# Block-selected causal attention feeding a gated convolution unit: convolution on four column groups of the array, fp16 high/low bounds, row-half scores, and a list-scheduled order

## The chip, the cores and the metric

The kernel runs on one NeuronCore of one Trainium2 chip. The metric is the device time of one execution in microseconds, the median over repeated executions. The profile gives the span from the first to the last instruction of one profiled execution, which is a little shorter than the time.

## The reference, cut to what matters

Inputs are `q`, `k`, `v` of shape (4, 8, 768, 64), a value matrix and an output matrix of 512 x 512, and a 5-tap depthwise filter `conv_w` (5, 512), all fp32. First comes attention with chunk selection: for each query, an upper bound of its score with each chunk of 32 keys is formed, and only the six chunks with the largest bounds take part. Its output `x` (4, 768, 512) then goes through a causal depthwise convolution, whose sigmoid gates `x @ w_val`, and through `w_out`.

```python
k_min, k_max = k_chunks.min(3), k_chunks.max(3)             # 24 chunks of 32 keys
ub = sum_d maximum(q * k_min, q * k_max)                    # (.., 768, 24), future chunks -1e9
top_chunks = argsort(ub)[..., -6:]
scores = q @ k.T / 8 ; masked to chosen chunks and to keys at or before the query
attn = softmax(scores) @ v
x = heads side by side                                      # (4, 768, 512)
gate = sigmoid(sum_k conv_w[k] * x shifted by k-4)
out = (gate * (x @ w_val)) @ w_out
```

## The kernel before, in words

Two heads make a pair, so there are 16 pairs (`NPAIR`), four per batch. The two heads of a pair lie side by side in the 128 partitions of transposed tiles: 64 rows of head dimension each.

Per pair the work is cut into steps, each a small function that issues its instructions:

- `kq_steps`: TensorE turns K and Q (fp32, 128 x 128 pieces, L155 and L178) so that the head dimension lies on the partitions; ScalarE writes fp16 copies with zero rows beside them (L159, L181, with GpSimd's casts L183); VectorE takes each chunk's maximum and minimum (L163, L164) and makes the small fp32 bound matrix `KB` (L167 to L172); GpSimd casts V (L190).
- `sel_steps`: the bounds are two fp32 matmuls per query tile of 128 (L207, L209), using `max(q*kmin, q*kmax) = q*kmin + relu(q)*(kmax-kmin)`; VectorE adds the causal fill, takes the top eight and compares with the sixth (L211 to L224); the "not chosen" matrix is turned (L233) and copied into spare rows of the query tile `QU` (L236).
- `attn_steps`: the scores are one matmul per head and key tile (L271, L291). The stationary operand holds 64 rows of keys and, in other rows, the chunk indicator times -30, so that the mask is added by the same matmul. It uses 88 or 128 rows of the array for one head at a time. ScalarE takes the exponential (L275, L295), GpSimd zeroes the upper triangle of diagonal blocks (L264, L280), TensorE multiplies by V with an extra column of ones (L304), VectorE normalises (L306, L307), and the result is turned into `xT` (L314, L316).
- `moe_gate`, `moe_val`, `moe_out`: for each of the 16 channel groups of 128 the depthwise convolution is done as matmuls with diagonal 128 x 128 matrices, five taps times a high and a low fp16 part, on each half of 384 positions: 20 matmuls (L334), then tanh (L339). The value product (L348), gating (L352), output product (L359), eviction (L362) and store (L363) follow per batch.

The order on every engine is the order in which the steps are issued. `merge` interleaves attention of pair i, selection of pair i+1, K/Q work of pair i+2 and the gate work of earlier pairs by equal fractions of each list:

```python
keyed += [((j + 0.5) / n, li, j, s) for j, s in enumerate(steps)]
...
merge(attn_steps(i),
      sel_steps(i + 1) if i + 1 < NPAIR else [],
      kq_steps(i + 2) if i + 2 < NPAIR else [],
      moe[i])
```

Loads of pair i+2 are issued ahead of each merge on the SyncE queue, 192 KB per head and tensor in rows of 256 bytes. Eight DMAs of this queue are in flight at most, since each waits for the one eight before it.

The softmax here doesn't subtract the row's maximum and nothing guards it: scores larger than these inputs give would overflow.

## Time and profile before

| quantity | value |
|---|---|
| time, median of 2 runs | 294.5 us (294.18 to 294.82) |
| span of the profiled execution | 292.5 us |
| mean granted TensorE clock | 0.959 |
| first score matmul (L271) starts | 27.07 us |
| last output matmuls (L359) start, span ends | 283.13 us, 292.5 us |
| DMA moved | 28.46 MB, queue 1 at 40.9% of 16 engines |
| convolution L334, busy | 57.8 us, 320 matmuls |
| bounds L207 and L209, busy | 31.2 and 32.3 us, 160 records each |
| scores L271, busy | 54.9 us, 224 matmuls |

A matmul's record includes the time in which it passes through the array, and records overlap, so a group's busy time and the mean of one matmul overstate what it costs in a stream. The distance from the start of one group to the start of the next is what the stream pays; the timeline gives it. Each engine works its own queue in order.

### The profile page before, as it was taken

The numbers are of one execution on the slowest core, as the hardware profiler recorded it, in microseconds if no ns is written. First come the engines' busy times: TensorE is split into PE (matmuls) and PEld (weight loads), VectorE is DVE, ScalarE is ACT, GpSimd is POOL, SyncE is SP. The second block draws the span as 40 slices with busy tenths as digits, with TensorE's granted clock in tenths as the row PEclk, the third lists the DMA queues.
The fourth block names the chain that finished last, engine by engine and source line by source line (L and its number), as shares of the span: only waits on it lengthen the run. The fifth ranks groups of instructions, "written<-read, shape, count | busy, mean of one in ns | idle before, by whom it ended". The sixth has DMA issues, their size and how long they took to land.

```text
span 292.5 us, 5928 instructions
## 1 busy us (share of the span) xinstructions
PE 241.3 (82%) x2161; PEld 171.6 (59%) x2161; DVE 155.2 (53%) x522; ACT 160.2 (55%) x329; POOL 121.8 (42%) x261
## 2 busy tenths in 40 slices
PE   2383926509998897999998999999989999999994
PEld 1181614405757575776666667676757676765551
DVE  3547162404676674858573657666645667631160
ACT  3232713503768659465674774756747765467313
POOL 2416189999254436243433253425251624223000
PEclk9999975956999999999999999999999999999999
DMA  7999992205162554242456343332211000003105
GB/s 165 211 304 245 218 175 54 54 0 110 33 132 55 110 110 99 66 108 56 107 151 159 91 114 86 70 87 61 74 74 38 36 2 0 2 2 143 73 2 215
DMA packets 80746, 28.46 MB, mean 97 GB/s; under 512 B 75962, under 2 KB 76622, under 8 KB 80718
## 3 DMA queue, kind: packets, MB, share of 16 engines
q1 hardware_dynamic: 80718, 28.09, 40.9%
q8 instruction: 17, 0.28, 0.4%
q14 instruction: 11, 0.09, 0.1%
HBM read 21.79 MB, written 6.29 MB: 96 GB/s over the span
## 4 chain that ended last, share of the span: by engine, by line
PE 66%; POOL 12%; ACT 10%; issue 3%; SPq 3%; DVE 2%; DMA 2%; ACTq 0%; POOLq 0%
PE ps_w L334 17%; PE ps_s L271 10%; POOL diag L379 7%; PE ps_av L304 6%; PE ps_w L348 6%; PE ps_w L359 6%; PE ps_w L209 6%; ACT P L275 5%; PE ps_w L207 5%; PE ps_w L155 4%; PE ps_w L178 2%; POOL QU L183 2%; PE ps_w L314 2%; ACT KE L159 2%; ACT osb L362 1%
## 5 line engine op out<-in xcount | busy, mean ns | idle before, releaser
L275 ACT ACTIVATE P<-ps_s 128x512 f16<-128x512 f32 x160 | 87.8, 606 | 57.1 <-PE ps_s L271 56.8
L271 PE MATMUL ps_s<-QU,KE 88*128 88x512 f16 (+5 forms) x224 | 54.9, 336 | 7.1 <-ACT P L275 4.1
L264 POOL TENSOR_SCALAR_AFFINE_SELECT P<-P 128x256 f16<-128x256 f16 (+1 forms) x80 | 29.0, 364 | 71.1 <-ACT P L275 58.3
L334 PE MATMUL ps_w<-xT,diag 128*128 128x384 f16 x320 | 57.8, 331 | 0.0
L304 PE MATMUL ps_av<-VA,P 128*128 128x65 f16 x672 | 33.4, 196 | 21.9 <-POOL P L264 19.9
L304 PEld LDWEIGHTS <-P 128*128 128x128 f16 x672 | 28.4, 99 | 32.0 <-POOL P L264 26.2
L159 ACT ACTIVATE KE<-ps_w 64x384 f16<-64x384 f32 x64 | 31.0, 485 | 26.9 <-PE ps_w L155 26.5
L183 POOL CAST QU<-q 64x384 f16<-64x384 f32 x64 | 35.1, 548 | 24.6 <-ACT q L181 22.7
L334 PEld LDWEIGHTS <-diag 128*128 128x128 f16 x320 | 31.0, 99 | 21.4 <-issue 1.9
L339 ACT ACTIVATE g<-ps_w 128x384 f32<-128x384 f32 x32 | 15.9, 498 | 30.5 <-PE ps_w L334 30.5
L209 PE MATMUL ps_w<-KB,q 128*128 128x48 f32 x160 | 32.3, 285 | 0.0
L163 DVE TENSOR_REDUCE kmx<-ps_w 128x12 f32<-128x384 f32 x32 | 17.8, 555 | 26.7 <-ACT KE L159 26.6
L236 DVE COPY QU<-ps_w 24x640 f16<-24x640 f16 x32 | 15.5, 484 | 29.9 <-PE ps_w L233 29.4
L207 PE MATMUL ps_w<-KB,rq 128*128 128x48 f32 x160 | 31.2, 278 | 0.0
L271 PEld LDWEIGHTS <-KE 88*128 88x128 f16 (+1 forms) x224 | 21.1, 101 | 16.8 <-issue 10.8
L280 POOL TENSOR_SCALAR_AFFINE_SELECT P<-P 128x256 f16<-128x256 f16 x32 | 13.1, 408 | 31.4 <-ACT P L275 31.3
L207 PEld LDWEIGHTS ps_w<-KB,rq 128*128 128x128 f32 x160 | 25.9, 202 | 0.3
L155 PE MATMUL ps_w<-ident,kn 128*128 128x128 f32 x96 | 17.7, 300 | 9.7 <-DMA kn<-in_k_dram 9.7
L209 PEld LDWEIGHTS ps_w<-KB,q 128*128 128x128 f32 x160 | 25.7, 202 | 0.0
L348 PE MATMUL ps_w<-xT,wval_sb 128*128 128x384 f16 x128 | 23.9, 325 | 1.8 <-ACT q L181 1.8
L190 POOL CAST VA<-vn 128x384 f16<-128x384 f32 x32 | 16.5, 516 | 20.4 <-PE ps_av L304 12.9
L359 PE MATMUL ps_w<-wout_sb,gv 128*128 128x512 f16 x96 | 23.8, 379 | 0.7 <-ACT osb L362 0.7
(46 smaller groups left out, 309.0 us busy)
## 6 DMA issues: line engine op xcount, KB each, us to landing
kn<-in_k_dram SPq DMA_DIRECT2D x32, 192.0 KB, 3.3
qn<-in_q_dram SPq DMA_DIRECT2D x32, 192.0 KB, 3.4
vn<-in_v_dram SPq DMA_DIRECT2D x32, 192.0 KB, 3.3
out_dram<-osb SPq DMA_DIRECT2D x24, 256.0 KB, 2.0
w<-in_moe_w_val_dram SPq DMA_DIRECT2D x1, 1024.0 KB, 5.6
w<-in_moe_w_out_dram SPq DMA_DIRECT2D x1, 1024.0 KB, 7.9
KE<-echunk SPq DMA_DIRECT2D x6, 96.0 KB, 2.7
cfill<-cfill SPq DMA_DIRECT2D x1, 120.0 KB, 2.3
```

What stands on the lines that cost most here:

```text
L155: nc.tensor.transpose(out=pt[:, tl * 128:(tl + 1) * 128], in_=kn[:, 3 * w + tl, :], identity=ident)
L159: nc.scalar.activation(out=ke[HP[hh], hh, sl], in_=pt[HP[hh]], func=AF.Copy, scale=0.125)
L183: nc.gpsimd.tensor_copy(out=qu[HP[hh], hh, sl], in_=q32[HP[hh], sl])
L207: nc.tensor.matmul(out=pu[:, it - 1, :], lhsT=rq[:, ts], rhs=kb[:, 0, :], start=True, stop=False)
L209: nc.tensor.matmul(out=pu[:, it - 1, :], lhsT=q32[:, ts], rhs=kb[:, 1, :], start=False, stop=True)
L264: nc.gpsimd.affine_select(out=ap, in_=ap, pattern=[[0, n], [1, 128]], compare_op=ALU.is_ge, fill=0.0, base=0, channel_multiplier=-1)
L271: nc.tensor.matmul(out=pq[:, col:col + n], lhsT=ke[KP[hh], hh, jt * 128:(jt + 1) * 128], rhs=qu[KP[hh], hh, q0:q0 + n], start=True, stop=True)
L275: nc.scalar.activation(out=pt, in_=pq, func=AF.Exp)
L304: nc.tensor.matmul(out=pav[:, qt, :], lhsT=where[hh, jt, qt], rhs=va[:, hh, jt, :], start=(jt == 0), stop=(jt == qt))
L334: nc.tensor.matmul(out=pg, lhsT=diag[:, ki * NCT + ct, part, :], rhs=xT[:, slot, w * HB + ki:w * HB + ki + HB], start=(n == 0), stop=(n == ...
L348: nc.tensor.matmul(out=pv, lhsT=wval_sb[:, ct, et * 128:(et + 1) * 128], rhs=xT[:, slot0 + ct, 4 + w * HB:4 + (w + 1) * HB], start=(ct == ...
L359: nc.tensor.matmul(out=po, lhsT=gv[b, et][:, s * 128:(s + 1) * 128], rhs=wout_sb[:, et, :], start=(et == 0), stop=(et == NCT - 1))
```

## The change

The change replaces the hand-written merge by a graph of operations with modelled durations and a list scheduler, and at the same time recasts three pieces of TensorE's work.

**Bounds.** Q is scaled by 64 and split into an fp16 high part `Qh` and low part `ql`; their positive parts are `rh` and `rl`. The bound matrix is split likewise, high and low side by side (96 columns). A query tile now takes four fp16 matmuls of 96 columns instead of two fp32 matmuls of 48. VectorE makes `ql`, `rh`, `rl` and adds the two halves of the product (`bsum`, twice); the bound matrix is made by seven small GpSimd instructions (`ksmall`).

**Scores.** The stationary operand holds only a head's 64 rows. Head 0 lies in rows 0 to 63 and head 1 in rows 64 to 127 of the array; their matmuls are issued in turn, to two banks. The mask is a second matmul from the indicator `E` and the turned selection `MT`, accumulated on the same bank, for queries from 192 on. ScalarE evicts K and Q with one instruction per half, both heads at once.

**Convolution.** A shifted copy of `xT` is made through DRAM: one DMA writes `xT` of a pair to `scr`, four DMAs read it into `XS` so that 32 channels lie in each quarter of the partitions, with the quarters holding shift and part (high or low) variants. A matmul then has 32 output columns, and the four groups of 32 channels go to four column groups of the array. Three shifts times four groups give 12 matmuls of 384 positions per half, 24 per pair instead of 20.

**Order.** Every operation has a key, `p * PERIOD + OFF[stage]`; on each engine the scheduler starts the ready operation with the smallest key, given modelled durations, a free bank of the eight, and the buffers of `NBUF`. The resulting order is what each engine's queue holds. Constants are made on the chip rather than loaded; the two weight matrices are loaded by GpSimd with a cast; eight matmuls on zeros are issued first.

In the resulting queues the first operations are these. SyncE: the loads of K, Q, V of pairs 0, 1 and 2, then the filter, then pair 3. TensorE: the zeros; K and Q of pairs 0 and 1; bounds of pair 0; K and Q of pair 2; bounds of pair 1; the turn of the filter; the turn of pair 0's selection; scores of pair 0. At the end, after the turn of the last pair's output, TensorE has 52 value matmuls, 96 convolution matmuls and 48 output matmuls left.

```diff
-    def merge(*lists):
...
+PERIOD = 9.537
+OFF = dict(load=-38.8, ktr=-26.25, qtr=-23.06, kev=-7.55, qev=-7.41, ksm=-26.91, spl=-1.52, vc=6.87,
...
+    def key(stage, p, x=0.0):
+        return p * period + off[stage] + x
...
+    G.op("cw", "SP", 2.0, kd + off["load"] + 2 * period, w_cw, w=[("cw4",)], lat=4.0)
...
+            G.op(f"{name}{p}", "SP", 1.1, key("load", p, x + (3 if x == 2 else 0)), load(name), w=[(name, p)], lat=3.2)
...
+        def rhi(p=p):
+            t.nc.vector.tensor_scalar(out=vv("rh", p), in0=vv("Qh", p)[:, 128:S], scalar1=0.0, scalar2=None,
+                                      op0=ALU.max)
+
+        def rlo(p=p):
+            t.nc.vector.scalar_tensor_tensor(out=vv("rl", p), in0=vv("Qh", p)[:, 128:S], scalar=0.0,
+                                             in1=vv("ql", p), op0=ALU.is_gt, op1=ALU.mult)
...
+                terms = [(vv("rh", p)[:, sl], 0), (vv("rl", p)[:, sl], 0), (vv("Qh", p)[:, sq], 1),
+                         (vv("ql", p)[:, sl], 1)]
+                for k, (lhsT, m) in enumerate(terms):
+                    t.nc.tensor.matmul(out=b[:, i * 96:(i + 1) * 96], lhsT=lhsT,
+                                       rhs=kb[:, m].rearrange("p a c -> p (a c)"), start=(k == 0), stop=(k == 3))
...
+                    for hh in range(2):
+                        nc.tensor.matmul(out=bb[hh][:, col:col + n], lhsT=kh[HP[hh], jt * 128:(jt + 1) * 128],
+                                         rhs=qh[HP[hh], q0:q0 + n], start=(si == 0), stop=(last and not masked),
+                                         skip_group_check=True)
+                    if masked:
+                        for hh in range(2):
+                            nc.tensor.matmul(out=bb[hh][:, col + m0 - q0:col + n],
+                                             lhsT=t.E[HP[hh], jt * 128:(jt + 1) * 128],
+                                             rhs=mt[HP[hh], m0 - 128:q0 + n - 128], start=False, stop=last,
+                                             skip_group_check=True)
...
+        def xw(p=p):
+            t.nc.sync.dma_start(out=t.scr[p % 4].rearrange("c (g n) -> g c n", g=4), in_=t.xT[:, p % 8, :])
+
+        def xs(p=p):
+            n = 4 * XW
+            for blk in range(4):
+                sh = 3 * (blk // 2)
+                t.nc.sync.dma_start(out=vv("XS", p)[32 * blk:32 * blk + 32, 0:n - 3], in_=t.scr[p % 4][:, sh:sh + n - 3])
...
+                for o in range(3):
+                    for g in range(4):
+                        t.nc.tensor.matmul(out=b[32 * g:32 * g + 32, 0:HB], lhsT=t.WD[:, o * 16 + (p % 4) * 4 + g, :],
+                                           rhs=x[:, g * XW + w * HB + o:g * XW + w * HB + o + HB], start=(o == 0), stop=(o == 2))
...
+    with tc.manual_schedule():
+        for o in order:
+            o.emit()
```

## The prediction

> **What bounds the kernel now.** I read the page first, for the engine that is busiest and for the chain that ended last.
>
> ```profile
> span 292.5 us, 5928 instructions
> PE 241.3 (82%) x2161; PEld 171.6 (59%) x2161; DVE 155.2 (53%) x522; ACT 160.2 (55%) x329; POOL 121.8 (42%) x261
> ...
> PE   2383926509998897999998999999989999999994
> ...
> PE 66%; POOL 12%; ACT 10%; issue 3%; SPq 3%; DVE 2%; DMA 2%; ACTq 0%; POOLq 0%
> ```
>
> TensorE is the bound: from about a third of the span on its slices are full, and it holds 66% of the chain. So the next question is what each kind of matmul costs there. For that I take the timeline of TensorE in the steady stage, and read the distance between starts, not the durations, which overlap.
>
> ```profile
> 157.29 2.28 PE L334 MATMUL ps_w<-xT,diag 128*128 128x384 f16 x13
> 159.41 0.50 PE L314 MATMUL ps_w<-identh,onat 128*128 128x128 f16 x6
> 159.74 0.38 PE L271 MATMUL ps_s<-QU,KE 88*128 88x512 f16 x1
> ...
> 160.51 0.32 PE L207 MATMUL ps_w<-KB,rq 128*128 128x48 f32 x2
> ...
> 162.68 1.03 PE L359 MATMUL ps_w<-wout_sb,gv 128*128 128x512 f16 x4
> 163.54 0.60 PE L271 MATMUL ps_s<-QU,KE 88*128 88x512 f16 x3
> 163.98 0.49 PE L155 MATMUL ps_w<-ident,kn 128*128 128x128 f32 x3
> 164.31 0.38 PE L271 MATMUL ps_s<-QU,KE 88*128 88x512 f16 x1
> ...
> 167.26 0.68 PE L304 MATMUL ps_av<-VA,P 128*128 128x65 f16 x16
> 167.78 0.38 PE L271 MATMUL ps_s<-QU,KE 128*128 128x512 f16 x1
> ```
>
> A convolution matmul takes (159.41 - 157.29)/13 = 163 ns, an fp16 turn 55 ns, one pair's bounds 162.68 - 160.51 = 2.17 us, an output matmul 215 ns, an fp32 turn 110 ns, an attention-times-V matmul 32.5 ns. Those of 384 and 512 columns come to 0.42 ns a column, and I use this for all wide ones. Per pair: turns of K and Q 12 x 0.11 = 1.32; bounds 2.17; turn of the selection 0.28; scores 5376 columns x 0.42 = 2.26; times V 42 x 0.0325 = 1.37; turn of the output 0.34; convolution 20 x 0.163 = 3.26; value 8 x 0.163 = 1.31; output 6 x 0.215 = 1.29. Sum 13.6 us. The chain in order of time gives the true period:
>
> ```profile
> 144.98 0.86 PE ps_w L359 x4
> ...
> 204.92 0.86 PE ps_w L359 x4
> ```
>
> These are the same step of two batches, four pairs apart: 59.94/4 = 14.98 us. So TensorE gives 13.6/14.98 = 0.91 of its time to the stream. I take this for the new kernel too; a planned order might do better, three nearly equal engines worse.
>
> The start is read from the timeline of the first 30 us.
>
> ```profile
> 14.19 0.88 PE L155 MATMUL ps_w<-ident,kn 128*128 128x128 f32 x3 [4.53 <-DMA kn<-in_k_dram]
> 24.12 2.07 POOL L366 CAST wval_sb<-w 128x2048 f16<-128x2048 f32 x1
> 24.36 2.04 DVE L185 TENSOR_SCALAR rq<-q 128x384 f32<-128x384 f32 x1
> 27.07 2.35 PE L271 MATMUL ps_s<-QU,KE 88*128 88x512 f16 x7 [1.86 <-DVE QU L236]
> ```
>
> TensorE stands 4.53 us for pair 1's keys while pair 0's bounds are queued behind them. The first score comes at 27.07. VectorE's L185, whose mean is 0.59 us, took 2.04 us beside a GpSimd cast.
>
> **What the Trainium skill says.** (1) TensorE: Matmul & The Clock Gate, Measured speedup vs the span model: four row tiles ran 3.07 times and three column tiles 2.38 times as fast as one after another. No matmul of this trace is tiled, so it neither confirms nor denies it. (2) TensorEngine Tiling (Array Packing), Key Properties: changing the tiling mode drains the engine. Not seen here either. (3) SBUF — State Buffer, Who interferes with whom: VectorE in a two-port mode, or with two inputs in SBUF against a GpSimd instruction that reads SBUF, waits until the other has ended. The 2.04 us beside the 2.07 us above agrees.
>
> **The change part by part.** All per pair on TensorE unless said.
>
> Bounds: 20 fp16 matmuls of 96 columns. Between 32.5 ns at 65 columns and 55 ns at 128 lies 44 ns, so 0.88 us for 2.17.
>
> Scores: 2688 columns per head as before, plus 2432 for the mask from query 192 on, 5120 per head. If the two row halves run side by side: 5120 x 0.42 = 2.15; one after another: 4.30; the skill's efficiency (about 0.8 of the tiles' number) would give 2.69. I take 2.2: its packs stood alone, so that fixed times weigh, while here matmuls follow in a stream.
>
> Convolution: 24 matmuls for 20. Four at a time: 24 x 0.163/4 = 0.98; at 3.07: 1.27; serial: 3.91. I take 1.0 for the same reason.
>
> Mode changes: the queue goes into and out of the row or column form some ten times a pair. A record of 331 ns at a distance of 163 says that about 0.17 us is passage through the array, so a drain costs 0 to 0.17: 0 to 1.7 a pair. I take 0.3, most being small beside the waits that the 0.91 already holds.
>
> The rest, unchanged: 1.32 + 0.28 + 1.37 + 0.34 + 1.31 + 1.29 = 5.91. Sum: 5.91 + 0.88 + 2.2 + 1.0 + 0.3 = 10.3 us against 13.6, or 165 us in all.
>
> The other engines, per pair. ScalarE: eight exponentials of 512, two of 384, two of 256, four evictions and two tanh of 384, one and a half evictions of 512. Five L275 in 2.56 us give 0.51 each back to back, and two L181 0.87, or about 0.4 each: in all 8.7; at record durations (606, about 500, 386 ns) 10.5. Splitting each head's K eviction (L159, 485 ns x4) is gone. VectorE: four reductions 2.2 (555 and 548 ns), `ql` 0.9, `rh` and `rl` 1.2, two sums 0.8 (L211 408 ns), ten MAX8 0.86, compare 0.43, selection copy 0.48, reciprocal and normalising 1.47, output copy 0.56, gating 1.09: 10.0 at record durations, about 8.7 back to back. GpSimd: about 4.8; seven small instructions of `ksmall` bounded by the 178 ns memset (L129, 96 columns) and the 294 ns select (L264, 128 columns) of the groups by shape. All lie beside TensorE as long as it is at 10.3. The new wait on GpSimd is for chunk maxima, with casts and triangles queued behind it; bounds wait for it two pairs ahead of need.
>
> DMA:
>
> ```profile
> 8.00:16.00 8.00, 2.89 (x13) 2.35 (x13) 2.98 (x10) 1.99 (x5) 3.16 (x6) 1.00 1.10 214
> ...
> 225.00:240.00 15.00, 14.52 (x141) 10.56 (x140) 8.60 (x28) 10.61 (x24) 6.54 (x15) 1.00 0.10 36
> ```
>
> The last two columns are the share of DMA time and GB/s. The 256-byte loads saturate at 214 GB/s, the stores' larger packets at 36/0.10 = 360. Loads 1.18 MB: 5.5 us; the copy through DRAM 0.99 MB: 2.75 at 360, 4.6 at 214; stores 0.39 MB: 1.1. Together 9.4 to 11.2, but loads are done well before the end, so it is hidden by 10.3/0.91 = 11.3.
>
> Start: before the filter stand 18 loads, 3.54 MB. At 214 GB/s they end near 17.5 us; at the rate at which pair 1's keys came (2.33 MB in 13 us, 180 GB/s) near 20.6. The turn of pair 2's keys and of the filter stand on TensorE ahead of pair 0's selection. The filter lands then at 20 to 22; with the turn, VectorE's split and the selection copy (about 2 us) the first score starts at about 24, 3 us earlier than now. Dropping 0.6 MB of constants is the gain; the order, planned with 1.1 us for two loads where 214 GB/s needs 1.8, gives much of it back. Before it TensorE has done 36 turns, two bounds, one selection: 6 us.
>
> End: after the last turn TensorE has 52 x 0.163 + 4 x 1.0 + 48 x 0.215 = 22.8 us of work, so the round trip through DRAM (two transfers of some 2 to 3.3 us each, by the rows of stores and loads) is hidden behind values and outputs. After the last output matmul there is an eviction and a store: now 292.5 - 288.3 = 4.2 us. The time is 2.0 over the span.
>
> Forecast: 24 + (165 - 6)/0.91 + 4.2 + 2.0 = 205 us.
>
> **Rivals.**
> A, tiles do not overlap: 10.3 - 2.2 - 1.0 + 4.30 + 3.91 = 15.3 a pair; (245 - 6)/0.91 + 30.2 = 293; with drains at 0.17 (another 1.4 a pair) 317, slower than before. For it: nothing in this trace runs two matmuls at once. Against: the skill's measurements.
> B, VectorE becomes the bound: record durations 10.0 plus 1 us of holding by GpSimd (three exposed instructions, about 0.3 each, as GpSimd is busy nearly half the time and an instruction lasts 0.4 to 1.0) is 11.0; less 14 us done before the first score and 4 in the tail, (176 - 18)/0.91 = 174; 24 + 174 + 22.8 + 6.2 = 227. For it: L185's 2.04 us. Against: in the busiest 30 us VectorE now does 21 us without being waited for.
> C, the planned order keeps TensorE fuller: perfect tiling, no drains, 0.95: 10.0 x 16 = 160; 154/0.95 + 30.2 = 192. For it: nothing wide is left in one piece. Against: the plan's load times are too short, and TensorE's queue waits in order for a late operand, as the 4.53 us show.
>
> **How the numbers follow.** Forecast 0.60, B 0.20, C 0.14, A 0.06. The likeliest is 205. The range goes from 188, a little under C, to 230, a little over B; only A and a few tails lie outside. Slower takes half of A and unknowns: 0.04; same the 293 side of A: 0.03; faster 0.93.
>
> **What would show it.** Right: distance between starts of two-head scores near 0.42 ns a column for both heads together; 12 convolution matmuls in 0.5 to 0.65 us; a pair's 20 bound matmuls in 0.9; period near 11.3; first score near 24 with TensorE waiting on the filter's load. Wrong: if the score group of a pair takes over 4 us (A), if TensorE waits mostly on VectorE (B), or if transfers through `scr` are what SyncE's queue waits for while loads stand behind them.

## The result, and the profile after

The changed kernel takes 235.9 us (median of 2 runs, 234.8 to 237.0), where the kernel before takes 294.5 us. The ratio is 0.800, with a 95% interval from 0.789 to 0.810. It is faster, as forecast, but 31 us slower than the 205 us forecast and outside the range of 188 to 230. The ratios in this document are formed from executions in the fast state alone, which matters most for the run with six output tiles, where three of six executions were slow and the fast ones took 231.4 to 233.9 us.

The page of the changed kernel: span, busy time of the engines, slices of TensorE, of its granted clock and of DMA, queue 1, and the chain that ended last.

```profile
span 233.1 us, 7133 instructions
...
PE 191.0 (82%) x2713; PEld 129.4 (56%) x2713; DVE 148.2 (64%) x481; ACT 142.7 (61%) x313; POOL 96.3 (41%) x216
...
PE   7476599999999994999991059999999999941993
...
PEclk9769779999999999799999558999999999995599
DMA  7999999989998999699999999596377845468133
...
q1 hardware_dynamic: 84288, 41.06, 81.5%
...
PE 45%; DVE 18%; DMA 18%; SPq 10%; issue 4%; ACT 3%; DVEq 0%; ACTq 0%
```

TensorE is still 82% busy, as it was before, but no longer full where it matters: its slices have a hole at slices 22 and 23 (122 to 134 us), another near the end and a short one at slice 16. DMA is full for nearly two thirds of the span, and the chain now goes through DMA and SyncE's queue for 28%, where before it was 5%, and through VectorE for 18%, where before it was 2%.

What TensorE's work costs is read from the starts in its timeline, as in the prediction:

```profile
36.11 0.51 PE L579 MATMUL b<-identh,on 128*128 128x128 f16 x6
...
44.87 0.51 PE L579 MATMUL b<-identh,on 128*128 128x128 f16 x6
...
53.45 0.51 PE L579 MATMUL b<-identh,on 128*128 128x128 f16 x6
...
110.86 1.17 PE L605 MATMUL b<-XS,WD 128*32 128x384 f16 x24
111.96 0.82 PE L628 MATMUL b<-xT,wval 128*128 128x384 f16 x4
...
122.48 0.39 PE L510 MATMUL b<-Qh,Kh 64*128 64x512 f16 x2
122.71 0.38 PE L515 MATMUL b<-MT,E 64*128 64x512 f16 x2
122.93 0.27 PE L510 MATMUL b<-Qh,Kh 64*128 64x256 f16 x2
...
136.63 0.26 PE L510 MATMUL b<-Qh,Kh 64*128 64x128 f16 x1 [13.16 <-ACT osb L658]
...
138.08 2.11 PE L605 MATMUL b<-XS,WD 128*32 128x384 f16 x24
```

Four column groups do run side by side: 24 convolution matmuls from 110.86 to 111.96, 1.10 us or 46 ns each, where one cost 163 ns. So do the row halves: two heads' matmuls of 512 columns take 122.71 - 122.48 = 0.23 us together, 0.45 ns a column for both heads. The turn of the output (L579), once per pair, comes 8.7 us apart early on. Then stands the hole of 13.16 us, and after it the record of the same 24 matmuls is 2.11 us long instead of 1.17: the granted clock has fallen to 5 tenths in the hole, and again in the long wait near the end (slices of PEclk above).

The windows of the same kernel: busy time and number of instructions of TensorE, its weight loads, VectorE, ScalarE and GpSimd; the last three columns are granted clock, share of DMA time and GB/s.

```profile
40.00:60.00 20.00, 19.07 (x351) 15.26 (x348) 19.79 (x66) 18.15 (x41) 12.88 (x31) 1.00 1.00 203
60.00:80.00 20.00, 19.61 (x351) 14.40 (x349) 19.59 (x71) 18.87 (x45) 14.29 (x30) 1.00 1.01 195
100.00:120.00 20.00, 20.00 (x288) 13.95 (x285) 16.25 (x48) 14.16 (x33) 8.86 (x23) 1.00 1.00 196
120.00:140.00 20.00, 6.71 (x62) 3.24 (x60) 2.95 (x15) 5.57 (x12) 1.71 (x2) 0.70 0.95 213
```

All sixteen DMA engines are taken, at about 200 GB/s, and go on being taken (0.95) while TensorE stands. From 40 to 80 us VectorE is the fullest compute engine, with 19.79 and 19.59 of 20 us. The hole's origin is on SyncE, whose queue holds loads, copies and stores in one order. Its timeline around the hole (columns: start, duration):

```profile
116.35 0.52 SPq L589 DMA_DIRECT2D scr<-xT  x1
116.98 2.39 SPq L354 DMA_DIRECT2D qn<-in_q_dram  x2
122.07 1.72 SPq L595 DMA_DIRECT2D XS<-scr  x4
...
128.14 0.52 SPq L589 DMA_DIRECT2D scr<-xT  x1
...
130.01 2.63 SPq L663 DMA_DIRECT2D out_dram<-osb  x2
134.08 1.72 SPq L595 DMA_DIRECT2D XS<-scr  x4
```

The copy's write is issued at 116.35 and two loads after it; then nothing more is issued until the reads of the copy start at 122.07, when the write has landed. The stores of two output tiles come out only at 130.01. ScalarE stands for them (`osb` has three tiles), and behind its evictions stand the exponentials whose banks the scores need:

```profile
135.99 1.31 ACT L658 ACTIVATE osb<-b 128x512 f32<-128x512 f32 x2 [13.85 <-DMA out_dram<-osb]
```

Over the whole execution SyncE waits most for the copy (line, what it waited for, total us, times, longest):

```profile
SPq L595 <- DMA scr<-xT: 45.1, 12, 5.6
```

And at the end TensorE waits for the last two copies, by its timeline:

```profile
206.45 1.17 PE L605 MATMUL b<-XS,WD 128*32 128x384 f16 x24 [0.96 <-DMA XS<-scr]
214.52 2.11 PE L605 MATMUL b<-XS,WD 128*32 128x384 f16 x24 [6.90 <-DMA XS<-scr]
216.56 5.91 PE L628 MATMUL b<-xT,wval 128*128 128x384 f16 x24
```

### The profile page after: what moved, and what is told of

Same layout as the page of the kernel before. It is cut to its first block, busy times and chain, and to the rows that moved or that the text cites. A ratio compares the mean times of both kernels' runs of the same rounds, so it can differ in the third digit from the quotient of the medians.

```text
span 233.1 us, 7133 instructions
## 1 busy us (share of the span) xinstructions
PE 191.0 (82%) x2713; PEld 129.4 (56%) x2713; DVE 148.2 (64%) x481; ACT 142.7 (61%) x313; POOL 96.3 (41%) x216
## 2 busy tenths in 40 slices
DMA packets 85377, 42.55 MB, mean 183 GB/s; under 512 B 77152, under 2 KB 80224, under 8 KB 85344
## 3 DMA queue, kind: packets, MB, share of 16 engines
q1 hardware_dynamic: 84288, 41.06, 81.5%
## 4 chain that ended last, share of the span: by engine, by line
PE 45%; DVE 18%; DMA 18%; SPq 10%; issue 4%; ACT 3%; DVEq 0%; ACTq 0%
PE b L628 9%; SPq L354 7%; PE b L605 7%; PE b L652 7%; DMA scr<-xT 5%; DMA qn<-in_q_dram 5%; PE b L365 5%; PE b L554 5%; DMA kn<-in_k_dram 4%; DVE km L377 4%; PE b L510 4%; DVE on L563 4%; PE b L451 3%; PE b L515 3%; DVE ql L415 2%
## 5 line engine op out<-in xcount | busy, mean ns | idle before, releaser
L524 ACT ACTIVATE P<-b 128x512 f16<-128x512 f32 (+1 forms) x192 | 88.3, 584 | 13.6 <-PE b L515 9.6
L532 POOL TENSOR_SCALAR_AFFINE_SELECT P<-P 128x512 f16<-128x512 f16 (+1 forms) x64 | 35.2, 570 | 53.5 <-ACT P L524 52.8
L510 PE MATMUL b<-Qh,Kh 64*128 64x128 f16 (+3 forms) x384 | 40.5, 269 | 13.3 <-ACT osb L658 13.2
L515 PE MATMUL b<-MT,E 64*128 64x128 f16 (+4 forms) x352 | 38.4, 266 | 1.3 <-DVE MT L496 1.3
L377 DVE TENSOR_REDUCE km<-b 128x12 f32<-128x384 f32 x64 | 33.0, 547 | 9.0 <-POOL P L532 3.8
L605 PE MATMUL b<-XS,WD 128*32 128x384 f16 x384 | 22.1, 358 | 7.9 <-DMA XS<-scr 7.9
L554 PE MATMUL b<-VA,P 128*128 128x65 f16 x672 | 26.7, 196 | 0.5 <-DVE on L563 0.3
L510 PEld LDWEIGHTS <-Kh 64*128 64x128 f16 x384 | 18.8, 97 | 12.4 <-issue 7.9
L628 PE MATMUL b<-xT,wval 128*128 128x384 f16 x128 | 25.6, 344 | 0.0
L652 PE MATMUL b<-wout,gv 128*128 128x512 f16 x96 | 22.2, 380 | 0.1
L407 ACT ACTIVATE Qh<-b 128x384 f16<-128x384 f32 x32 | 14.7, 499 | 11.4 <-PE b L365 11.3
## 6 DMA issues: line engine op xcount, KB each, us to landing
scr<-xT SPq DMA_DIRECT2D x16, 193.5 KB
```

What stands on the lines that cost most here:

```text
L377: t.nc.vector.tensor_reduce(out=vv("km", p)[:, i, w * 12:(w + 1) * 12], in_=bank(("kn", p, w))[:, 0:HB].rearrange("p (c t) -> p c t", t=CH ...
L510: nc.tensor.matmul(out=bb[hh][:, col:col + n], lhsT=kh[HP[hh], jt * 128:(jt + 1) * 128], rhs=qh[HP[hh], q0:q0 + n], start=(si == 0), stop= ...
L515: nc.tensor.matmul(out=bb[hh][:, col + m0 - q0:col + n], lhsT=t.E[HP[hh], jt * 128:(jt + 1) * 128], rhs=mt[HP[hh], m0 - 128:q0 + n - 128], ...
L524: t.nc.scalar.activation(out=t.P[p % 2][hh][bi], in_=bank(("s", p, bi, hh))[:, 0:n], func=AF.Exp, scale=0.125 / QS)
L532: t.nc.gpsimd.affine_select(out=ap, in_=ap, pattern=[[0, n], [1, 128]], compare_op=ALU.is_ge, fill=0.0, base=0, channel_multiplier=-1)
L554: t.nc.tensor.matmul(out=b[:, qt, :], lhsT=t.P[p % 2][hh][bi][:, col:col + 128], rhs=vv("VA", p)[:, hh, jt, :], start=(jt == 0), stop=(jt ...
```

## The experiments

After this profile there are two theories. **Bandwidth:** the copy through DRAM and the 256-byte loads together need nearly all the time of the DMA engines, and everything late follows from that. **Order:** the engines' time would do, but the plan believes the copy's write to take 2.6 us, it takes 5 to 6, and SyncE's queue stands behind it with loads and stores. A narrower form of the second is that the stores and the three output tiles make the loss.

I use one sum beside the time: the DMA time of an execution, that is the shares of all queues times the span. For the changed kernel the queues' shares are 81.5 + 2.8 + 0.7 + 0.2 = 85.2%, times 233.1 = 199 us.

### Stores and output tiles

Six output tiles instead of three:

```diff
-        return a[v % nbuf[name]]
+        return a[v % len(a)]
...
-    t.tiles = {n: [tl(f"{n}{i}", *sh) for i in range(nbuf[n])] for n, sh in shapes.items()}
+    t.tiles = {n: [tl(f"{n}{i}", *sh) for i in range(6 if n == "osb" else nbuf[n])]
+               for n, sh in shapes.items()}
```

> The changed kernel in the same planned order, with six instead of three output tiles, so that an output eviction on ScalarE does not wait for the store of the tile three before it. Theory Q (SyncE's one queue in order: reads of the shifted copy wait for its write, stores and loads stand behind them, and ScalarE and TensorE wait for a store): the 13 us hole near 124 us closes and little comes back: 219 to 224 us against 235.9. Rival B (the 16 DMA engines are saturated, so any wait taken away comes back at a load): 231 us or more. Rival O (the planned order is wrong for the compute engines, DMA only by chance at the end of the wait): no change, 234 or more.

Measured: 234.65 us, ratio 0.787 (0.781 to 0.793). The interval overlaps that of the changed kernel, so nothing can be told from it; the 219 to 224 us of the first theory did not come. And the stores on ScalarE's queue, with three tiles:

```diff
-                t.nc.sync.dma_start(out=t.out[b_, s * 128:(s + 1) * 128, :], in_=vv("osb", 6 * b_ + s))
+                t.nc.scalar.dma_start(out=t.out[b_, s * 128:(s + 1) * 128, :], in_=vv("osb", 6 * b_ + s))
```

> The changed kernel in the same order, with the output stores issued from ScalarE's queue right after the eviction instead of SyncE's. Same bytes, same buffers. Theory Q: stores no longer stand behind reads that wait for the write, so the hole near 124 us closes: 219 to 225 us. Rival B: 231 or more. Rival O: 234 or more.

Measured: 237.4 us, ratio 0.807 (0.802 to 0.813). TensorE's waits and SyncE's in this kernel:

```profile
PE b L605 <- DMA XS<-scr: 18.7, 6, 5.6
```

```profile
SPq L595 <- DMA scr<-xT: 57.9, 12, 7.0
```

The hole behind the stores is gone and the loss has moved: TensorE now waits 18.7 us for the copies themselves. The narrow form of the order theory falls: it expected 219 to 225 us.

### The write of the copy left out

```diff
-            t.nc.sync.dma_start(out=t.scr[p % 4].rearrange("c (g n) -> g c n", g=4), in_=t.xT[:, p % 8, :])
+            if p < 4:
+                t.nc.sync.dma_start(out=t.scr[p % 4].rearrange("c (g n) -> g c n", g=4), in_=t.xT[:, p % 8, :])
```

> The changed kernel without the write of the shifted copy for pairs 4 to 15; its reads stay, with the same bytes, and take what pairs 0 to 3 left in DRAM. Left out: the gates of pairs 4 to 15 come from stale data. Of 2.57 MB per pair only 0.2 MB goes (8%), but the reads no longer wait for a write. Theory Q: both the hole near 124 us and most of the 8 us wait in the last 30 us close: 208 to 216 us. Rival B: 8% less DMA at most, 228 us or more. Rival O: 234 or more.

Measured: 215.8 us, ratio 0.734 (0.730 to 0.738), 20 us less. The DMA time falls by only 5 us, from 199 to 193.5 (90.4% of 214.0), so most of these 20 us are not the write's own bandwidth. The traces show where they go: TensorE's waits for the copies at the end, 7.9 us, are gone, and the hole is 4.4 us long instead of 13.2, which is 16.7 of the 19.1 us of span. Here the order theory has its best support.

### Wider rows for the loads

Loads in 1536-byte rows instead of 256, with the same bytes, DMAs and order. The positions then lie elsewhere in the tile, and in the second form the two heads are mixed as well, so these kernels do the same work on inputs in the wrong places: they price the rows and are no replacement. A first form permuted only the DRAM side:

```diff
-                                        in_=src[b_, h0 + hh].rearrange("(t p) d -> p t d", p=128))
+                                        in_=src[b_, h0 + hh].rearrange("(p t) d -> p t d", p=128))
```

> The changed kernel with Q, K and V loaded in rows of 1536 bytes instead of 256: same bytes, same number of DMAs and same waits, only fewer and larger packets. The positions come in another order within a head, so the result is that of permuted inputs; no work is left out. At the 360 GB/s of large packets the loads of a pair take 3.3 us of DMA time instead of 5.5. Rival B: 205 to 212 us, and DMA share falls to about 0.75. Theory Q: the writes that the reads wait for land sooner (about 3 us instead of 6), so part of the holes closes: 215 to 224. Rival O: 233 or more.

Measured: 237.9 us, ratio 0.809 (0.803 to 0.815). A miss that tests nothing. Its page shows that the packets stayed narrow, since the tile still keeps the two heads of a position side by side:

```profile
DMA packets 85377, 42.55 MB, mean 181 GB/s; under 512 B 77152, under 2 KB 80224, under 8 KB 85344
```

The second form makes the tile's side one piece as well:

```diff
-                    t.nc.sync.dma_start(out=vv(name, p)[:, :, hh * 64:(hh + 1) * 64],
-                                        in_=src[b_, h0 + hh].rearrange("(t p) d -> p t d", p=128))
+                    t.nc.sync.dma_start(out=vv(name, p).rearrange("p t d -> p (t d)")[:, hh * HB:(hh + 1) * HB],
+                                        in_=src[b_, h0 + hh].rearrange("(p t) d -> p (t d)", p=128))
```

> e3_wide left the packets at 256 bytes, since the tile's rows were still split by head; here the tile side is made contiguous too, so that Q, K and V come in packets of 1536 bytes. Bytes, DMAs, waits and order as in the changed kernel; the values are those of permuted inputs, no work is left out. Theory W (SyncE's one queue is the bound: about 6 us of issuing a pair plus 4 to 5 us of standing for the write of the shifted copy): the write lands sooner behind shorter loads, at most half of the 45 us of standing goes: 222 to 230 us. Rival B (DMA engines saturated): the loads' DMA time falls from 5.5 to about 3.3 us a pair and the time with it: 205 to 215.

Measured: 206.25 us, ratio 0.704 (0.701 to 0.707), 30 us less, as the theory of bandwidth expected. Its page, its windows and SyncE's longest wait:

```profile
DMA packets 23937, 42.55 MB, mean 206 GB/s; under 512 B 3424, under 2 KB 18784, under 8 KB 23904
...
q1 hardware_dynamic: 22848, 41.06, 67.9%
```

```profile
40.00:60.00 20.00, 19.39 (x355) 15.52 (x355) 19.58 (x63) 18.43 (x44) 13.89 (x30) 1.00 0.89 251
60.00:80.00 20.00, 19.62 (x353) 13.78 (x351) 19.83 (x71) 18.53 (x44) 14.00 (x33) 1.00 0.77 213
100.00:120.00 20.00, 19.52 (x313) 13.82 (x306) 14.18 (x42) 14.48 (x34) 6.86 (x15) 1.00 0.92 280
```

```profile
SPq L595 <- DMA scr<-xT: 62.2, 16, 5.1
```

The same megabytes take 148.6 us of DMA time (72.0% of 206.4 us) instead of 199. SyncE's queue holds the same order, and SyncE waits for the write even longer than before, 62.2 us; yet TensorE waits for a copy only once, 6.3 us for that of the last pair. So before the end the wait costs time only where the DMA engines have none left to catch up. The Trainium skill's DMA: Bandwidth & Descriptors, Specifications, gives 512 bytes as the least transfer for line rate; this pair of runs agrees as far as it goes: 203 GB/s at a full share against 251 at a share of 0.89 in the same window; no run has loads of a width between the two.

Both edits together, permuted loads and no write from pair 4 on:

> Both e2_nowait and e5_wide at once: no write of the shifted copy for pairs 4 to 15 (left out: their gates come from stale data) and 1536-byte packets for the loads. It asks what of the 215.8 us of e2_nowait was still DMA bandwidth. Theory W with the start bound by the loads (11.6 us of waits for K and Q in e2_nowait): 205 to 209. Rival B: 200 or less. If the compute engines bind: 213 or more.

Measured: 196.9 us, ratio 0.671 (0.669 to 0.672). This too is what the theory of bandwidth expected, and about what the changed kernel takes when DMA holds nothing up: TensorE waits 1.1 us for keys and for no query or copy. Of the 9.4 us that leaving out the write gives here, 6.3 are the last pair's wait.

### The plan told of the true latency

```diff
-        G.op(f"xw{p}", "SP", 0.55, key("xs", p), xw, r=[("xT", p)], w=[("scr", p)], lat=2.6)
-        G.op(f"xs{p}", "SP", 2.2, key("xs", p, 0.1), xs, r=[("scr", p)], w=[("XS", p)], lat=4.6)
+        G.op(f"xw{p}", "SP", 0.55, key("xs", p), xw, r=[("xT", p)], w=[("scr", p)], lat=6.0)
+        G.op(f"xs{p}", "SP", 2.2, key("xs", p, 0.1), xs, r=[("scr", p)], w=[("XS", p)], lat=6.0)
```

> The changed kernel with two numbers of the plan changed: the write of the shifted copy is planned with 6.0 us to landing instead of 2.6, its reads with 6.0 instead of 4.6. Same instructions, same bytes; the plan puts three loads instead of one or two between a write and its reads. Theory W: SyncE stands for the write less than 20 us in all instead of 45: 216 to 223 us. Rival B: 231 or more.

Measured: 226.0 us, ratio 0.768 (0.765 to 0.772), between the two expectations, though SyncE's wait for the write fell to 15.9 us as the order theory had it. Ten microseconds come from the order alone, by changing two figures. A hole of 10.4 us before the scores, behind the stores, is left. With the stores on ScalarE's queue and six output tiles as well:

> The plan with 6.0 us for the copy's write and reads, and now stores on ScalarE's queue and six output tiles as well. The plan alone gave 226.0 us and left a hole of about 10 us in which output matmuls wait for output tiles whose stores stand behind the copy in the queue. If that hole is lost time: 214 to 220. If the DMA engines are the limit, it only moves: 223 to 228.

Measured: 221.7 us, ratio 0.752 (0.747 to 0.757): between the two expectations. And with all DMA figures of the plan set to what the trace shows, stores on ScalarE's queue and six output tiles included:

```diff
-            G.op(f"{name}{p}", "SP", 1.1, key("load", p, x + (3 if x == 2 else 0)), load(name), w=[(name, p)], lat=3.2)
+            G.op(f"{name}{p}", "SP", 1.8, key("load", p, x + (3 if x == 2 else 0)), load(name), w=[(name, p)], lat=5.5)
...
-        G.op(f"xw{p}", "SP", 0.55, key("xs", p), xw, r=[("xT", p)], w=[("scr", p)], lat=2.6)
-        G.op(f"xs{p}", "SP", 2.2, key("xs", p, 0.1), xs, r=[("scr", p)], w=[("XS", p)], lat=4.6)
+        G.op(f"xw{p}", "SP", 0.8, key("xs", p), xw, r=[("xT", p)], w=[("scr", p)], lat=6.0)
+        G.op(f"xs{p}", "SP", 2.6, key("xs", p, 0.1), xs, r=[("scr", p)], w=[("XS", p)], lat=6.0)
...
-            G.op(f"od{b_}.{s}", "SP", 0.6, key("ev", p3, x), outdma(s), r=[("osb", 6 * b_ + s)], lat=2.2)
+            G.op(f"od{b_}.{s}", "SP", 0.6, key("ev", p3, x), outdma(s), r=[("osb", 6 * b_ + s)], lat=4.0)
```

> The full-size copy; only the plan's DMA figures are replaced by what the trace of the changed kernel shows (loads 1.8 us apart and 5.5 us of latency, copy 0.8 and 2.6 us apart with 6.0 us, stores 4.0 us), stores on ScalarE's queue, six output tiles. Theory bandwidth: the engines stay full, so at best the 226 of the longer copy latency alone: 220 to 230. Theory order (a plan that knows the true DMA times would hide the copy): under 215.

Measured: 228.9 us, ratio 0.778 (0.774 to 0.782). A truer plan is not a better one here: TensorE then waits 14.7 us for keys that come later. The orders tried here get back at most 14 of the 39 us that lie between 235.9 and 196.9.

### The convolution undone

The rest of the change stays; the convolution is again 20 full-array matmuls per pair from `xT`, and there is no copy.

```diff
-                for o in range(3):
-                    for g in range(4):
-                        t.nc.tensor.matmul(out=b[32 * g:32 * g + 32, 0:HB], lhsT=t.WD[:, o * 16 + (p % 4) * 4 + g, :],
-                                           rhs=x[:, g * XW + w * HB + o:g * XW + w * HB + o + HB], start=(o == 0), stop=(o == 2))
+                for o in range(10):
+                    k = o // 2
+                    t.nc.tensor.matmul(out=b[:, 0:HB], lhsT=t.WD[:, (p % 4) * 10 + o, :],
+                                       rhs=t.xT[:, p % 8, w * HB + k:w * HB + k + HB], start=(o == 0), stop=(o == 9))
...
```

> One part undone: the convolution as in the kernel before, 20 matmuls a pair on the whole array from the transposed tile itself, in the list-scheduled kernel with all other parts. No shifted copy, no write and reads through DRAM. TensorE's stream grows by 3.26 - 1.09 = 2.2 us a pair, 35 us. Theory W: the standing goes, so the 35 us are paid only in part, 228 to 240 us, about what the changed kernel takes. Rival O (the order is at fault for the compute engines): 250 or more.

Measured: 236.3 us, ratio 0.806 (0.802 to 0.810): the same as the changed kernel. Page and timeline of TensorE:

```profile
PE 215.6 (92%) x2649; PEld 146.4 (62%) x2649; DVE 147.7 (63%) x473; ACT 143.2 (61%) x313; POOL 116.6 (50%) x252
...
q1 hardware_dynamic: 78750, 25.18, 48.5%
```

```profile
113.65 3.43 PE L585 MATMUL b<-xT,WD 128*128 128x384 f16 x20
116.92 0.81 PE L608 MATMUL b<-xT,wval 128*128 128x384 f16 x4
```

Twenty matmuls in 116.92 - 113.65 = 3.27 us against 1.10: the column groups save 2.17 us a pair, 35 us in all, on TensorE, and what comes with the copy gives all of it back. (The kernels differ in more than that: the plan was made anew, and GpSimd, which makes 40 diagonal matrices here, is busy 38.0 of the 40 us from 30 to 70 us.) This run also prices the copy: queue 1 takes 0.485 x 234.3 = 114 us without it and 0.815 x 233.1 = 190 with it, so (190 - 114)/16 = 4.8 us a pair. In the packet records of the changed kernel the copy's own packets take 4.1 us a pair; the rest is mostly the 256-byte packets of the loads, which take 22.7 ns each there and 20.7 here.

### The copy at half its bytes

`XS` holds every channel four times: shifts 0 and 3, each twice, once for the high and once for the low part of the filter. The low part needs no copy of its own. So rows 0 to 63 now hold the first half of the positions, rows 64 to 127 the second, and the parts become separate matmuls of 64 rows and 32 columns: 48 in eight tiles.

```diff
-                sh = 3 * (blk // 2)
-                t.nc.sync.dma_start(out=vv("XS", p)[32 * blk:32 * blk + 32, 0:n - 3], in_=t.scr[p % 4][:, sh:sh + n - 3])
+                o = (blk // 2) * n + 3 * (blk % 2)
+                t.nc.sync.dma_start(out=vv("XS", p)[32 * blk:32 * blk + 32, 0:n - 3], in_=t.scr[p % 4][:, o:o + n - 3])
...
+            for k in range(6):
+                part, o = k // 3, k % 3
+                for g in range(4):
+                    for w in range(2):
+                        t.nc.tensor.matmul(out=bb[w][32 * g:32 * g + 32, 0:HB],
+                                           lhsT=t.WD[HP[w], part * 48 + o * 16 + (p % 4) * 4 + g, :],
+                                           rhs=x[HP[w], g * XH + o:g * XH + o + HB], start=(k == 0), stop=(k == 5))
```

Here `n = 4 * XH` with `XH = HB + 6`; the write goes out in two DMAs, one per half of the positions, and the filter's tile `WD` is twice as large.

> The copy is read back into the partitions at half the bytes: rows 0 to 63 of XS hold the first half of the positions with shifts 0 and 3, rows 64 to 127 the second half, and the filter's high and low parts go from the rows into two matmuls each; 48 matmuls of 64 x 32 in eight tiles (two row halves times four column groups) take the place of 24 of 128 x 32. Same result, same order otherwise. Theory bandwidth (the copy and the loads together fill the DMA engines): 0.40 MB less a pair, at about 200 GB/s 2.0 us of a pair's some 11, so 16 to 30 us less than the changed kernel: 206 to 220 us. Theory wait (the reads wait for the write of the copy, whatever their size): the wait of 5 to 6 us stays, 228 to 236. If eight tiles do not run side by side, a half's matmuls cost 1.1 us more a pair on TensorE, seen in the trace as over 2 us for the 48.

Measured: 209.6 us, ratio 0.711 (0.706 to 0.716), 26 us less than the changed kernel, with nothing of the computation left out. Page, TensorE's timeline, and SyncE's longest wait:

```profile
PE 186.4 (89%) x3097; PEld 129.0 (62%) x3097; DVE 148.4 (71%) x485; ACT 140.8 (68%) x313; POOL 99.9 (48%) x220
...
q1 hardware_dynamic: 86400, 34.79, 72.1%
```

```profile
111.04 1.17 PE L609 MATMUL b<-XS,WD 64*32 64x384 f16 x48
112.14 0.84 PE L555 MATMUL b<-VA,P 128*128 128x65 f16 x21
```

```profile
SPq L598 <- DMA scr<-xT: 19.4, 17, 3.0
```

The 48 matmuls take 1.10 us, as the 24 did. Queue 1 takes 150 us instead of 190. The hole is gone, with the plan's wrong latencies left as they were: the theory of bandwidth gives the number, the theory of the wait alone does not. The bytes are not all that changed, though. The plan was made anew with the convolution as one operation, and between a write and its reads SyncE's queue now has four loads instead of two for pairs 5 and 6, and two instead of four for pairs 0 and 2. SyncE's wait for the write has fallen to 19.4 us, at most 3.0, although the packets of a write still last 2.6 to 4.1 us. How much of the 26 us belongs to that order is not shown. With the better plan, stores on ScalarE's queue and six output tiles on top:

> The half-size copy together with a plan that expects 6.0 us for the write and the reads, stores on ScalarE's queue and six output tiles. Theory bandwidth plus late copy (both add up): 195 to 208 us. If the wait is all that matters, about the 226 of the plan with 6.0 us alone.

Measured: 207.9 us, ratio 0.705 (0.701 to 0.710), inside the first expectation, but it can't be told from the run without these three. What they were worth with full DMA engines (14 us) is gone once the engines have room.

### The copy's write on all engines

One thing was still open: why does the write of 193 KB take 5 to 6 us, and does it matter? In the trace of the changed kernel the 128 packets of a write (1548 bytes, about 90 ns each) last 2.7 to 4.3 us, and in the mean of a write 2.5 to 3.8 of them are under way (3.8 is the highest mean, not the highest number at a time). The Trainium skill's DMA: Bandwidth & Descriptors, Why a DMA increments its semaphore by 16 and not by 1, says that a DMA is shared by the largest number of engines up to 16 that divides the slowest dimension on both sides. The write's DRAM side begins with the four groups, `"c (g n) -> g c n"`, so by that rule four engines carry it. Written as four DMAs of 32 channels, with nothing else changed:

```diff
-            t.nc.sync.dma_start(out=t.scr[p % 4].rearrange("c (g n) -> g c n", g=4), in_=t.xT[:, p % 8, :])
+            for g in range(4):
+                t.nc.sync.dma_start(out=t.scr[p % 4][:, g * XW:(g + 1) * XW], in_=t.xT[32 * g:32 * g + 32, p % 8, :])
```

> The write of the copy as four DMAs of 32 channels each instead of one whose outer dimension is the four groups; same bytes, same reads, same plan. In the trace of the changed kernel the 128 packets of a write last 2.7 to 4.3 us and at most 3.8 of them run at a time, as if four of the sixteen engines carried it. Theory four engines: the write spread over all of them lands in about 3 us instead of 5 to 6, SyncE's wait for it falls from 45 to under 25 us, and the time goes most of the way to that of the kernel without the write (216): 216 to 224 us. Rival, the bandwidth in sum: the engines are as full as before, the wait is mostly queueing: 230 to 236 us.

Measured: 226.8 us, ratio 0.769 (0.765 to 0.773). Page and SyncE's wait for the write:

```profile
DMA packets 86338, 42.56 MB, mean 189 GB/s; under 512 B 78112, under 2 KB 81184, under 8 KB 86304
```

```profile
SPq L596 <- DMA scr<-xT: 10.9, 12, 2.6
```

The changed kernel has 77152 packets under 512 bytes, the same number as the page of the first row experiment shows above. The 960 more are packets of 4 bytes (3105 and 4065 in the two traces), and one for each engine of a DMA would be just that: 16 writes times (4 x 16 - 4) = 960. In the mean 4.3 to 9.5 packets of a write are now under way. So the write did go through four engines, and now goes through sixteen. It is waited for 2.6 us at most instead of 5.6, and 10.9 us in all instead of 45.1. Yet the time falls by only 9 us, outside both expectations: a hole of 11.6 us and a wait of 4.7 for the last pair's copy stay, though SyncE hardly waits for the write any more. The same with a copy laid out in DRAM in 128 rows, one write and reads in shorter pieces:

```diff
-            t.nc.sync.dma_start(out=t.scr[p % 4].rearrange("c (g n) -> g c n", g=4), in_=t.xT[:, p % 8, :])
+            t.nc.sync.dma_start(out=t.scr[p % 4], in_=t.xT[:, p % 8, :])
...
-                t.nc.sync.dma_start(out=vv("XS", p)[32 * blk:32 * blk + 32, 0:n - 3], in_=t.scr[p % 4][:, sh:sh + n - 3])
+                t.nc.sync.dma_start(
+                    out=vv("XS", p)[32 * blk:32 * blk + 32, :].rearrange("c (g n) -> c g n", g=4)[:, :, 0:XW - 3],
+                    in_=t.scr[p % 4].rearrange("(g c) n -> c g n", g=4)[:, :, sh:sh + XW - 3])
...
```

> The copy laid out in DRAM as it lies in the tile, 128 rows: one write DMA with 128 rows as its outer dimension, and the reads take four pieces of 1.5 KB per partition instead of one of 6 KB. Theory four engines: as with four DMAs, 214 to 224 us, if the smaller pieces of the reads cost nothing. Rival, the bandwidth in sum: 230 to 238 us.

Measured: 225.1 us, ratio 0.766 (0.764 to 0.768): the same, and again outside both expectations. And this layout with the copy at half its bytes:

> The copy at half its bytes together with the 128-row layout, so that the write is one DMA of 1.5-KB rows and the reads have pieces of 0.8 KB. The half-size copy alone gave 209.6 us. Theory four engines: 200 to 206 us, with SyncE's wait for the write under 10 us instead of 19. Rival, the bandwidth in sum: 207 to 212 us.

Measured: 205.3 us, ratio 0.698 (0.695 to 0.701), 4 us less than the half-size copy alone and inside the range of the theory of four engines. Its mechanism isn't shown: SyncE's wait for the write is 16.7 us and not under 10, and the longest is 3.8 us where it was 3.0. TensorE's waits for copies (1.2 us) and for an output tile (1.3) are gone; where the rest comes from stays open. It is the fastest kernel here that leaves nothing out, 31 us faster than the changed one. Stores on ScalarE's queue and six output tiles on top:

> The same with stores on ScalarE's queue and six output tiles. If nothing but TensorE is left as the bound: 197 to 203 us, near the 196.9 of the run with neither narrow loads nor late write. If the loads of 256 bytes still hold it up: 204 to 209 us.

Measured: 206.2 us, ratio 0.701 (0.699 to 0.704), no gain, as expected if the loads of 256 bytes still hold it up. TensorE is 90% busy in both; the waits left that are longest are for keys and queries, 5.4 and 2.9 us in the kernel of 205.3, against 1.1 and none listed in the run with wide loads and no write.

## Why the prediction was wrong, point by point

**Right: the price of TensorE's work.** Bounds: in the trace of the changed kernel the starts of L451 lie 0.04 us apart, as estimated. Scores: 0.45 ns a column for both heads, 2.3 us for 5120 columns where the forecast has 2.2. Convolution: 1.10 us for 1.0. Rival A, that tiles do not overlap, is out. The drains weren't measured apart; the convolution's 1.10 us against 24 x 0.163/4 = 0.98 leave 0.12 us for going into its form and out of it.

**Right over the whole, wrong for one stage: the other engines lie beside it.** VectorE is 64% busy, TensorE's waits for it are 1.3 us and less, and with DMA out of the way the kernel takes 196.9 us, so rival B's 227 is out. But from 40 to 80 us VectorE is busy 39.4 of 40 us, the chain that ended last lies on it for most of that stage, and the turns of the output come 8.5 to 8.8 us apart whether the DMA engines are full (starts 36.11, 44.87, 53.45) or not (30.53, 39.06, 47.64 with wide rows). Rival B's sum without the gating, which comes later, is 10.0 - 1.1 = 8.9 us a pair; the forecast took TensorE to be the bound in every stage. No run takes work off VectorE, so that it sets the pace there is read from the traces alone. The bound's wait on GpSimd for chunk maxima counts for little: TensorE waits 0.3 us for `KB`, and 3.7 in the run with DMA out of the way.

**Right in kind, off in size: the start.** The first score comes at 20.30 us, not 24; TensorE waits for the filter's load 0.8 us, which lands a little early, at 19.8. The first scores carry no mask and so do not wait for the selection copy that the forecast put before them; only the masked ones do, at 22.22.

**Wrong: the DMA step.** It said "Together 9.4 to 11.2 … so it is hidden by 10.3/0.91 = 11.3". Both sides of the comparison failed. The sum is 190/16 = 11.9 us a pair. By the packet records of the changed kernel the term that was mis-sized is the loads, 6.5 us a pair for 5.5; the copy's 4.1 lies within its 2.75 to 4.6, and the stores take the 1.1 of the forecast. Part of that is a misreading: the 214 GB/s of the loads stood beside a share of 1.10, and their packets in the trace of the kernel before, 20.0 ns each, come to 5.8 us a pair. With that the forecast's own upper sum is 11.5 and no longer fits into 11.3. The rest comes with fuller engines: a 256-byte packet takes 20.7 ns in the kernel without the copy and 22.7 in the changed one. And the period to hide it in was an average over the whole kernel: early on, with convolution, values and outputs not yet begun, the kernel goes at 8.7 us a pair (L579 above), and that is when the loads are wanted. Sixteen pairs at 11.9, plus weights, are 199 us of DMA time, as much as the whole forecast span of 203; a resource of that size cannot be called hidden. That it also lies in one in-order queue with a wait in it made it worse: the engines were used for 85% of the span only.

**Wrong: the end.** "The round trip through DRAM … is hidden behind values and outputs." The last write took 5.99 us and the last reads 4.55 (chain of the changed kernel), not 2 to 3.3 each, and the convolution of the last pair stands in TensorE's queue ahead of 32 of the value matmuls that were to hide it. That write was issued at 202.57, 8 us after the turn that it needs (194.15), since SyncE stood for the write of the pair before and then issued its reads. Cost: 7.9 us of waiting, and about 3 more because the 48 matmuls after it run at the lower clock (214.52 to 222.30).

**What DMA costs in all.** Against the run with neither narrow loads nor late write, whose span is 195.0 and whose TensorE is busy for 181.4 us, the changed kernel's span is 38.1 us longer. Of these 191.0 - 181.4 = 9.6 are TensorE's records getting longer, which fits the lower granted clock after holes, and 28.5 are idle time: the hole 13.2, the copies at the end 7.9, and keys and queries (5.6 + 4.7, of which 1.1 is there in the other run too) 9.2, together 30.3, with some smaller waits shorter. When it is lost is seen from the turns of the output beside the kernel with wide rows, whose order is the same: the changed kernel is 5.6 us behind at the first (36.11 and 30.53), 5.8 at the sixth (79.19 and 73.37), 11.5 at the eighth (101.92 and 90.46), 26.2 at the tenth, after the hole (143.21 and 116.96), and 26.0 at the last (194.15 and 168.13). So full DMA engines cost nothing for long stretches: they cost at the start, at one late load of queries and in the hole.

The compute part of the forecast was 8 us too high and the DMA part about 39 too low. That 196.9 is near rival C's 192 does not speak for C: in that run the first score comes at 17.7 us, 6.3 earlier than forecast, and from it to the end of the time 179 us pass, where the forecast has 181. That the factor 0.91 fits so well is partly luck, since it was taken from the kernel before: here it is made of a stage that VectorE holds and of one in which TensorE is full (20.00 of 20 us from 140 to 160 in that run).

**Which of the two theories.** Bandwidth is the larger cause: widening the loads takes away 30 us with the queue in the same order and a longer wait for the write in it. Halving the copy takes away 26, with a somewhat changed order. The order theory is right in part: with full engines, less waiting gives back some 10 us, whether the plan is told of it (226.0) or the write is given all engines (226.8), and 20 when the write is left out, because only then are the waits at the end gone too. With wide rows, leaving it out gives 9.4, most of it at the end; with the copy at half its bytes, a better plan or a write on all engines gives 2 to 4. These figures do not add up, since the waits stand in one another's shadow.

The prediction named this outcome as what would prove it wrong, "if transfers through `scr` are what SyncE's queue waits for while loads stand behind them", but made no rival of it and gave it no time.

## What to carry to other kernels

Add up the DMA time of all queues over the whole kernel, each width of packet at the rate that a trace shows for it at a full share, and compare it with the new span and with the period of the fastest stage, not with a mean period; if it is near, expect DMA to hold the kernel up, and a faster engine to stand the longer. Look at the other engines by stages too: a mean of 64% hid a stage in which VectorE was full. A copy that buys TensorE time must be priced per byte: here 2.17 us a pair gained cost 4.8 us of DMA. Before reordering a queue around a slow transfer, make the transfer smaller, its rows longer, and see that its outermost dimension lets all engines share it.

## What the runs showed of the hardware

- Eight tiles of 64 rows by 32 columns run side by side with little loss: 48 matmuls of 384 columns in 1.10 us, 23 ns each, against 46 ns with four column groups of full height and 163 ns one at a time. That is 7.1 and 3.6 times. The Trainium skill's TensorE: Matmul & The Clock Gate, Measured speedup vs the span model, has 2.38 for three column tiles and 3.07 for four row tiles, beside a model of the span of one pack, and no row for these two forms; in a stream they came nearer to the number of tiles.
- A packet is as long as the shorter piece of the two sides: permuting the DRAM side alone left 77152 packets under 512 bytes, with both sides in one piece 3424 were left. A load's packet of 256 bytes took 22.7 ns in the changed kernel, one of 1536 bytes 74.7 ns in that with wide rows: six times the bytes in 3.3 times the time.
- One DMA with an outer dimension of 4 runs on four engines: its 128 packets took 2.7 to 4.3 us, and SyncE, with the reads behind it, waited up to 5.6 us; as four DMAs of 32 rows, on sixteen engines, 1.2 to 2.8 us and up to 2.6 us.
